# Fixed places for every tile in a two-layer decode kernel: three slots and a ring, a half-wise feed-forward, and 192 KB kept across the layers

## The chip, the core and the metric

The kernel runs on one core of a Trainium2 chip. TensorE (PE in the profile) multiplies, VectorE (DVE), ScalarE (ACT) and GpSimd (POOL) do the rest, and SyncE (SP) issues nearly all loads from HBM into the on-chip memory, which has 128 partitions. Sixteen DMA engines carry them. A "KB" below is a KB per partition unless "in all" stands beside it. The metric is the device time of one execution in microseconds; less is better.

## The reference

Two batch rows, one new token each, go through attention with a long cache, a gated feed-forward, and then through both a second time with the same weights and caches. Everything is float32.

```
B, Sq, D = 2, 1, 512;  Hq, Hkv, Sk, Dh = 32, 8, 32768, 128;  F = 1792
A(x): q = (x @ wq) as 32 heads; k, v repeated 4 times over the heads
      p = softmax(q . k * Dh**-0.5);  o = p . v;  return o @ wo
B(x): gate = x @ W_gate; up = x @ W_up; gate = gate * (gate > 0)
      return (gate * up) @ W_down
x = A_x
x = x + A(layernorm(x));  x = x + B(layernorm(x))
x = x + A(layernorm(x));  x = x + B(layernorm(x))
```

The keys take 268 MB and the values 268 MB, and each of the two layers reads them, so that nearly all bytes are caches.

## The kernel before, in words

A layer has 16 turns, one for each pair of a key head and a batch row (`NG`). A turn has a key half and a value half of 128 KB each. Either is cut in 8 pages of 16 KB, and 4 pages are one slot of 64 KB. `keys(i)` (L394) multiplies the queries with the 8 key pages of turn i (`k_tile`, L218, 8 products of 512 columns for a page), `soft_max` (L226) and `soft_tail` (L241) make the weights and turn them, and `values(i)` (L419) multiplies them with the 8 value pages (`v_tile`, L297 to L309) into one PSUM tile, `acc`. `evacuate` (L313) scales and copies it, `head_out` (L322) folds it into `oT`, and every second turn `project` (L331) multiplies a pair of heads with 8 KB of `wo` into the PSUM tile `op`, in 16 products of 128 columns (`spread`, L164). The program order is keys(i), then values(i-1) (L456 to L458), so the loads of a turn's keys are issued ahead of the values of the turn before. Layer 0 takes the turns upward and layer 1 downward: the last turn of layer 0 is the first of layer 1, and its keys (128 KB) and 56 KB of its values (pages 4, 5, 6 and half of page 3, `KEPT_PAGES` and `KEPT_PART`, L37 and L38) stay on the chip.

All data lie in one tile of 221 KB, `arena`, cut in units of 1 KB. `take` (L62) hands out a run of free units: for a load the one that has been free longest by the program's order, for a working tile the one nearest the top. So where a tile lies follows from the whole order of takes and `done` calls (L79). A load waits on SP until the last reader of its units has finished, and all later loads stand behind it on SP's queue. Most cache loads are whole slots (`pages`, L94, with `whole`); the values of turns 14 and 15 and some pages at the layers' border come as single pages (L437 to L438), the last page of turn 15 in four pieces of 4 KB.

The side load: of turn 14's page 3 the last 3 of 8 column blocks (6 KB) are not loaded with the page. They come from an array `side`, packed as rows, by two DMAs of 20 partitions with 20 KB each, whose source has an outermost dimension of 5 (`load_side`, L288 to L293, `SIDE_ENGINES`, L44). `side_keys` (L258) regroups the weights for it and `v_side` (L276) multiplies 10 chunks. The load is issued after page 3 and ahead of page 4 (L446 to L449).

Between the layers the work is one chain: the last value pieces, `evacuate`, `head_out`, `project` (L463), the addition to x (`add`, L168), then `feed_forward` (L337): `centred` (L143), 8 loads of 7 KB of gate and up weights with products of 448 columns (L345), `variance` (L153, four products), the gate's relu on ACT (L356), product and transposes on DVE, then 6 loads of down weights (8, 8, 4, 4, 2, 2 KB; `DOWN`, L39), whose first 8 blocks go into a PSUM tile of their own, `dn` (L371), that is copied (L378) and folded into `tot` (L381). `queries` (L175) of the next layer follows, with 8 loads of 8 KB. Its products are interleaved with the first products of the kept keys (L190). The free space for all these loads is what the 184 KB kept leave. At the end of layer 1 nothing is kept, and the weights are loaded ahead into free slots.

Of the kernel before, what the change touches and what calls it, by code (L numbers as in the profile page):

```python
# [12 lines left out]
P = 128  # L13
D = 512
# [12 lines left out]


PIECE = 256
PAGE = 4096  # L30
HALF = 4
UNITS = 221
TOP = 192
SCRATCH = 64


KEPT_PAGES = (4, 5, 6)  # L37
KEPT_PART, KEPT_FROM = 3, 4  # L38
DOWN = (4, 4, 2, 2, 1, 1)  # L39


SIDE_TURNS = (14,)
SIDE_PAGE, SIDE = HALF - 1, 3
SIDE_ENGINES, SIDE_ROWS, SIDE_CHUNKS, SIDE_GAP = 5, 20, 5, 64  # L44
# [5 lines left out]
def attention_reglu_decode(ctx: ExitStack, tc: tile.TileContext, x, k, v, wq, wo, wgu, wd, consts, side, out):  # L50
# [6 lines left out]

    arena = sb.tile([P, UNITS * PIECE], F32, name="arena")
    freed = [0] * UNITS
    clock = [0]  # L60

    def take(width, top=True, tile=True):  # L62
        n = -(-width // PIECE)
        step = min(8, 1 << (n - 1).bit_length()) if n < 64 else n
        runs = [
            (top and u < TOP, 0 if tile else max(freed[u : u + n]), -u if n < 16 else u, u)
            for u in range(0, UNITS - n + 1, step)
            if None not in freed[u : u + n]
        ]
        u = min(runs)[-1]  # L70
        freed[u : u + n] = [None] * n
        return arena[:, u * PIECE : u * PIECE + width], range(u, u + n)

    def load(src, top=False):
        t = take(src.shape[-1], top, False)
        nc.sync.dma_start(t[0], src)
        return t

    def done(loaded):  # L79
        clock[0] += 1  # L80
        for u in loaded[1]:
            freed[u] = clock[0]


    def blocks(src, size, order, per):
        for at in range(0, len(order), per):
            t, us = load(src[:, order[at] * size : (order[at] + per) * size])
            for e in range(per):
                yield t[:, e * size : (e + 1) * size], us if e == per - 1 else ()

    def page(src, n, j):
        return load(src[n, j // HALF, :, j % HALF * PAGE : (j % HALF + 1) * PAGE])

    def pages(src, n, whole):  # L94
        for h in range(NT // HALF):
            if whole:
                t, us = load(src[n, h])
                for j in range(HALF):
                    yield t[:, j * PAGE : (j + 1) * PAGE], us[16 * j : 16 * j + 16]
            else:  # L100
                for j in range(HALF):
                    yield page(src, n, HALF * h + j)


# [17 lines left out]
    nc.gpsimd.memset(qz, 0.0)  # L122
    qT = sb.tile([P, HKV * REP, NB], F32, name="qT")
# [8 lines left out]
    ring = sb.tile([P, 32], F32, name="stat")  # L132
    turn = [0]

    def one(n=1):
        at = turn[0]
        turn[0] = (at + 2) % 32
        return ring[:, at : at + n]

    def centred(total, name):  # L143
        mp = small(f"mean{name}")
        nc.tensor.matmul(mp[:, :32], total.to_broadcast([P, P]), means, start=True, stop=True)  # L145
        xT, sq = take(P), take(P)
        nc.vector.transpose(xT[0], xq)
        rows = xT[0].rearrange("p (a b) -> p a b", b=32)
        nc.vector.tensor_tensor(rows, rows, mp[:, None, :32].to_broadcast([P, KT, 32]), ALU.subtract)
        nc.vector.tensor_tensor(sq[0], xT[0], xT[0], ALU.mult)  # L150
        return xT, rows, sq

    def variance(sq, name):  # L153
        vp = small(f"var{name}")
        for kt in range(KT):
            nc.tensor.matmul(vp[:, :NB], mean.to_broadcast([P, P]), sq[0][:, kt * 32 : kt * 32 + NB],
                             start=kt == 0, stop=kt == KT - 1)
        done(sq)
        ve = one(NB)
        nc.vector.tensor_scalar_add(ve, vp[:, :NB], EPS)  # L160
        return ve

# [10 lines left out]


    def queries(L, total, first, between):  # L175
        xt, xT, sq = centred(total, f"a{L}")
# [3 lines left out]
        order = [B * KT + kt for B in (front, 1 - front) for kt in range(KT)]  # L180
        parts = blocks(wq, 4 * D, order, 1 if L else 2 * KT)
        for B in (front, 1 - front):
            for kt in range(KT):
                t = next(parts)
                for c in range(4):
                    nc.tensor.matmul(qp[32 * c : 32 * c + 32, B, :], xT[:, kt, :], t[0][:, c * D : (c + 1) * D],  # L186
                                     start=kt == 0, stop=kt == KT - 1)
                done(t)
                if B != front and kt:
                    next(between, None)  # L190
                if B == front and kt == 0:
                    ve = variance(sq, f"a{L}")
                    nc.gpsimd.tensor_tensor(rq, ve, mhalf, ALU.pow)
                    nc.vector.tensor_scalar_mul(rq, rq, DH ** -0.5)
            q = take(D)
            qs = q[0].rearrange("p (a b) -> p a b", b=32)
            nc.vector.transpose(q[0], qp[:, B, :])
            for b in range(NB):
                nc.vector.tensor_scalar_mul(qT[:, 16 * B : 16 * B + 16, b], qs[:, :, b], rq[:, b : b + 1])
            done(q)  # L200
            if B == front:
                place_queries(0, first)
        done(xt)
# [4 lines left out]

# [16 lines left out]

    def soft_max(L, n):  # L226
# [3 lines left out]
        mt = take(32)  # L230
        nc.vector.tensor_scalar_mul(mt[0], pair, m1[:, 0:1])  # L231
        nc.tensor.matmul(mp[:, :32], same, mt[0], start=True, stop=True)  # L232
        done(mt)
        nm = one()
        nc.vector.tensor_reduce(nm, mp[:, :32], AX.X, ALU.max, negate=True)  # L235
        p = take(2 * D)
        rs = one()
        nc.scalar.activation(p[0], sc_of[n].rearrange("p a b -> p (a b)"), AF.Exp, bias=nm[:, 0:1], scale=1.0, accum_out=rs)  # L238
        red_of[n] = (p, rs)

    def soft_tail(L, n, aside=False):  # L241
        p, rs = red_of.pop(n)
        pT = take(2 * D)
        for B in range(2):
            nc.vector.transpose(pT[0][:, B * D : (B + 1) * D], p[0][:, B * D : (B + 1) * D])  # L245
        if aside:
            side_of[n] = side_keys(p[0])
        done(p)
# [8 lines left out]

    def side_keys(p):  # L258
        W = SIDE_CHUNKS * 32
        t = take(2 * W)  # L260
        at = SIDE_PAGE // 2 % 2 * D + (SIDE_PAGE % 2 * 8 + 8 - SIDE) * 32

        def windows(rows):
            return bass.AP(rows.tensor, rows.offset + at, [rows.ap[0], [SIDE_ROWS, SIDE_CHUNKS], [1, 32]])

        def chunks(rows):
            return rows.rearrange("p (k r) -> p k r", r=32)

        nc.gpsimd.memset(t[0][64:, W:], 0.0)
        nc.vector.transpose(chunks(t[0][:, :W]), windows(p))  # L270
        for c in (0, 32):
            nc.vector.transpose(chunks(t[0][c : c + 32, W:]), windows(p[64 + c : 96 + c]))
        nc.vector.tensor_scalar_mul(t[0], t[0], side_rows[:, 0:1])
        return t

    def v_side(n, vt):  # L276
        t = side_of.pop(n)
        J = SIDE_PAGE // 4
        for k in range(2 * SIDE_CHUNKS):
            nc.tensor.matmul(  # L280
                acc[32 * (k % 4) : 32 * (k % 4) + 16, :],
# [108 lines left out]
    for L in range(NLAYER):  # L390
# [3 lines left out]
        def keys(i):  # L394
# [8 lines left out]
            for j, t in enumerate(loads):  # L403
# [5 lines left out]
                if last and i == 0:  # L409
                    yield  # L410
# [112 lines left out]
```

## Time and profile before

| | |
|---|---|
| median of 3 runs | 2583.39 us (2583.19 to 2585.2) |
| profiled execution: its own time, its span | 2585.52 us, 2583.7 us |
| instructions in the trace | 20190 |
| PE, DVE, ACT busy | 1322.4, 148.4, 40.9 us |
| HBM read | 1105.39 MB, 428 GB/s over the span |
| granted TensorE clock, mean | 0.746 |

The span is what the profiler saw of the program's instructions; the execution's own time is 1.8 us longer. Each query of the trace gives rows. A row of the timeline has the start and length in us, the engine and line, the operation, its output and inputs, the number of instructions merged, and in brackets the idle time before them and what ended it. "SPq" is SP's queue of issues. A row of the windows has the bounds and the length, the busy time of each engine with its instructions, the granted clock, the share of time in which the 16 DMA engines were busy, and what they moved. Every float32 product counts as two matmul instructions.

### The profile page before, as it was taken

What the parts mean: (1) busy time and instruction counts of PE and PEld (TensorE: products, weight loads), DVE (VectorE), ACT (ScalarE), POOL (GpSimd) and SP (SyncE); (2) the same over time, 40 slices, a digit from 0 to 9 for tenths busy, and PEclk for the clock granted to TensorE, in tenths of its full rate; (3) what the DMA queues carried; (4) which work ended last, traced back from release to release, by engine and by line L of the source; (5) the groups of instructions that cost most, each with busy time, mean ns of one, the idle gap of its engine ahead of it and who ended that gap; (6) DMA issues with size and microseconds to landing.
All of it is one profiled execution on the core that took longest, in us unless ns stands there. A gap on an engine that the chain in (4) does not pass through costs nothing.

```text
span 2583.7 us, 20190 instructions
## 1 busy us (share of the span) xinstructions
PE 1322.4 (51%) x9588; PEld 351.7 (14%) x9588; DVE 148.4 (6%) x357; ACT 40.9 (2%) x67; POOL 2.4 (0%) x10
## 2 busy tenths in 40 slices
PE   3554554455455445545685454445445544554465
PEld 1111111111111111111121111111111111111111
DVE  0000000000000000000010000000000000000000
ACT  0000000000000000000000000000000000000000
POOL 0000000000000000000000000000000000000000
PEclk9777777777777777777777777777777777777787
DMA  9999999999999999999999999999999999999999
GB/s 423 436 426 433 436 430 433 437 428 435 431 436 427 436 437 427 434 434 403 414 387 438 428 433 435 434 430 436 431 430 437 433 426 437 435 430 434 431 424 376
DMA packets 31446, 1106.75 MB, mean 428 GB/s; under 512 B 3500, under 2 KB 3764, under 8 KB 6836
## 3 DMA queue, kind: packets, MB, share of 16 engines
q1 hardware_dynamic: 31204, 1105.34, 99.5%
q8 instruction: 75, 1.23, 0.2%
q10 hardware_dynamic: 160, 0.12, 0.0%
q14 instruction: 7, 0.06, 0.0%
HBM read 1105.39 MB, written 0.07 MB: 428 GB/s over the span
## 4 chain that ended last, share of the span: by engine, by line
DMA 69%; PE 22%; another core or an unknown queue 8%; DVE 0%; issue 0%; ACTq 0%; SPq 0%; POOL 0%; DVEq 0%; POOLq 0%
DMA arena<-k 45%; DMA arena<-v 21%; PE sc L218 14%; PE acc L304 5%; DMA cst<-consts 1%; DMA arena<-wgu 1%; PE qp L186 1%; PE po L326 1%; DMA arena<-wq 1%; PE op L166 1%; PE gu L345 0%; PE dn L371 0%; PE mp L232 0%; PE sm L250 0%
## 5 line engine op out<-in xcount | busy, mean ns | idle before, releaser
L304 PE MATMUL acc<-arena 128*16 128x512 f32 (+1 forms) x4116 | 593.0, 727 | 598.5 <-DMA arena<-v 598.5
L218 PE MATMUL sc<-arena,qz 128*32 128x512 f32 x4096 | 591.6, 730 | 592.6 <-DMA arena<-k 592.6
L218 PEld LDWEIGHTS sc<-arena,qz 128*32 128x32 f32 x4096 | 143.4, 130 | 987.8 <-issue 664.9
L304 PEld LDWEIGHTS acc<-arena 128*16 128x16 f32 x4116 | 118.5, 109 | 1023.1 <-issue 512.4
L228 DVE TENSOR_REDUCE stat<-sc 128x1 f32<-128x1024 f32 x32 | 39.2, 1225 | 662.4 <-PE sc L218 662.4
L238 ACT ACTIVATE arena<-sc,stat 128x1024 f32<-128x1024 f32 x32 | 35.6, 1113 | 2360.2 <-DVE stat L235 2308.2
L320 DVE TENSOR_SCALAR arena<-acc,stat 128x512 f32<-128x512 f32 (+1 forms) x38 | 24.8, 665 | 810.6 <-PE acc L304 810.6
L245 DVE STREAM_TRANSPOSE arena<-arena 128x512 f32<-128x512 f32 x64 | 41.5, 687 | 2.4 <-ACT arena L238 2.4
L326 PE MATMUL po<-cst,arena 128*128 128x4 f32 x256 | 34.7, 258 | 2.1 <-DVE arena L320 2.1
L326 PEld LDWEIGHTS po<-cst,arena 128*128 128x128 f32 x256 | 31.9, 195 | 26.7 <-issue 23.5
L252 DVE RECIPROCAL stat<-sm 128x1 f32<-128x1 f32 x32 | 5.3, 166 | 415.4 <-PE sm L250 415.4
L345 PE MATMUL gu<-arena 128*32 128x448 f32 x128 | 22.7, 836 | 9.5 <-DMA arena<-wgu 9.2
L235 DVE TENSOR_REDUCE stat<-mp 128x1 f32<-128x32 f32 x32 | 6.1, 191 | 350.1 <-PE mp L232 350.1
L186 PE MATMUL qp<-arena 128*32 128x512 f32 x128 | 22.7, 822 | 5.7 <-DMA arena<-wq 3.0
L166 PE MATMUL op<-arena,oT 128*2 128x128 f32 x512 | 18.3, 287 | 4.1 <-DVE oT L329 4.1
L232 PEld LDWEIGHTS mp<-arena,cst 128*128 128x128 f32 x64 | 13.1, 256 | 52.1 <-issue 49.6
L145 PE MATMUL meana<-cst,stat 128*128 128x32 f32 x4 | 1.0, 341 | 35.5 <-DMA cst<-consts 35.0
L232 PE MATMUL mp<-arena,cst 128*128 128x32 f32 x64 | 16.9, 353 | 3.5 <-DVE arena L231 3.5
L250 PEld LDWEIGHTS sm<-stat,cst 128*128 128x128 f32 x64 | 9.5, 188 | 28.4 <-issue 28.4
L166 PEld LDWEIGHTS op<-arena,oT 128*2 128x2 f32 x512 | 12.3, 87 | 6.4 <-DVE oT L329 5.5
L250 PE MATMUL sm<-stat,cst 128*128 128x1 f32 x64 | 12.2, 260 | 0.0
L329 DVE COPY oT<-po 128x4 f32<-128x4 f32 x32 | 5.1, 161 | 76.4 <-PE po L326 76.4
(56 smaller groups left out, 94.1 us busy)
## 6 DMA issues: line engine op xcount, KB each, us to landing
arena<-v SPq DMA_DIRECT2D x31, 2048.0 KB, 27.7
arena<-wo SPq DMA_DIRECT2D x16, 1024.0 KB, 51.2
arena<-k SPq DMA_DIRECT2D x8, 2048.0 KB, 16.8
arena<-wq SPq DMA_DIRECT2D x8, 1024.0 KB, 8.5
arena<-wgu SPq DMA_DIRECT2D x8, 896.0 KB, 7.9
arena<-wgu SPq DMA_DIRECT2D x4, 1792.0 KB, 21.0
arena<-v SPq DMA_DIRECT2D x8, 512.0 KB, 34.2
arena<-wd SPq DMA_DIRECT2D x4, 1024.0 KB, 8.7
```

Source lines behind the costliest of these rows:

```text
L166: nc.tensor.matmul(tot[32 * c : 32 * c + rows.shape[-1], :P], rows, w[:, c * P : (c + 1) * P], start=start, stop=stop)
L186: nc.tensor.matmul(qp[32 * c : 32 * c + 32, B, :], xT[:, kt, :], t[0][:, c * D : (c + 1) * D], start=kt == 0, stop=kt == KT - 1)
L218: nc.tensor.matmul(sc_of[n][32 * c : 32 * c + 32, B, :], qz[:, i % 2, 28 - 4 * j : 60 - 4 * j], kt[:, ch * D : (ch + 1) * D], start=j == 0 ...
L228: nc.vector.tensor_reduce(m1, sc_of[n], AX.XY, ALU.max)
L232: nc.tensor.matmul(mp[:, :32], same, mt[0], start=True, stop=True)
L238: nc.scalar.activation(p[0], sc_of[n].rearrange("p a b -> p (a b)"), AF.Exp, bias=nm[:, 0:1], scale=1.0, accum_out=rs)
L245: nc.vector.transpose(pT[0][:, B * D : (B + 1) * D], p[0][:, B * D : (B + 1) * D])
L250: nc.tensor.matmul(sm[:, 0:1], same, rs, start=True, stop=True)
L304: nc.tensor.matmul(acc[32 * c : 32 * c + 16, e * w : (e + 1) * w], pT[:, B, m, 16 * J : 16 * J + 16], vt[:, at * D + e * w : at * D + (e + ...
L320: nc.vector.tensor_scalar_mul(acs[:, at : at + w], acc[:, at : at + w], linv[:, 0:1])
L326: nc.tensor.matmul(po[:, :REP], acs[0][:, t * P : (t + 1) * P], selh[:, 4 * t : 4 * t + 4], start=t == 0, stop=t == 3)
L345: nc.tensor.matmul(gu[32 * j : 32 * j + 32, s, :FS], xT[:, kt, :], t[0][:, j * FS : (j + 1) * FS], start=kt == 0, stop=kt == KT - 1)
```

## The change

The allocator is gone, and each tile has a written place. Units 0 to 191 are three slots of 64 KB, taken in rotation by whole loads, and units 192 to 220 are a ring of 29 KB with one fixed place for each working tile. `home(s, p)` is a page's place in a slot. The other parts:

- Kept across the layers: pages 3 to 6 whole (64 KB) beside the 128 KB of keys. All three slots are then full, and the weights between the layers (`wgu`, `wd`, `wq`, the last `wo`) stream through the ring alone, in places that come round every three loads.
- The values of turns 13, 14 and 15 come as pages; in layer 0, turns 14 and 15 use one slot for both halves. The second key half of turn 15 comes in two loads of 32 KB.
- The side load moves to turn 13 and comes as four DMAs of 25 partitions with 8 KB each, one for each 32 partitions, again with an outermost dimension of 5; its place is ring units 16 to 23. Four chunks are multiplied, not ten.
- `project` makes 4 products of 512 columns for the first 7 pairs; `gather` folds their sum once a layer.
- `feed_forward` works in two column halves: gate and up of half 0, its relu, product and transposes, then half 1; the down weights go straight into `tot` (8, 6, 8, 4, 2 KB), and `variance` is one product after the gate and up products.

The diff, cut: most removed lines stand in the listing above.

```diff
+KB = 256
+SLOT, RING, ARENA = 64, 192, 221
+KEPT_PAGES = (3, 4, 5, 6)
+DOWN = ((4, 3), (4, 2, 1))
+SIDE_TURN = NG - 3
+SIDE_PAGE, SIDE = 3, 3
+SIDE_WAYS, SIDE_ROWS, SIDE_CHUNKS, SIDE_GAP = 5, 25, 4, 64
...
+    def take_slot():
+        s = next_slot[0]
+        next_slot[0] = (s + 1) % 3
+        return s
+
+    def whole(src, n, cut=1):
         for h in range(NT // HALF):
...
+            s, m = take_slot(), cut if h else 1
+            for e in range(m):
+                t = load(slot(s, e * SLOT // m, HALF * PAGE // m), src[n, h, :, e * HALF * PAGE // m : (e + 1) * HALF * PAGE // m])
+                for j in range(HALF // m):
+                    yield t[:, j * PAGE : (j + 1) * PAGE]
...
+    P_AT, ACS_AT, SIDE_KEYS_AT, SUM_AT, SIDE_AT, WO_AT, MT_AT, XT_AT = 8, 12, 14, 14, 16, 20, 28, 28.5
+    G_AT, H_AT, HT_AT, SQ_AT, Q_AT, LAST_ACS_AT = 0, 0.875, (1.75, 2.625), 3.5, 0, 4
+    LAST_AT = (4, 8, 12, 16)
+    GU_AT = ((6, 13, 20, 6), (13, 20, 6, 13))
+    DOWN_AT = ((20, 6), (12, 20, 24))
+    WQ_AT = (4, 8) + (12, 20, 4) * 3
+
+    def pT_at(i):
+        return 0 if i % 2 else 4
...
+    nc.gpsimd.memset(ring(P_AT, (WO_AT + 8 - P_AT) * KB), 0.0)
...
+        for at, (B, kt, cs, t) in enumerate(blocks):
+            if t is None:
+                lo = (B * KT + kt) * 4 * D + cs[0] * D
+                t = load(ring(WQ_AT[at], len(cs) * D), wq[:, lo : lo + len(cs) * D])
...
+    def v_side(L, n):
+        vt = ring(SIDE_AT, SIDE_CHUNKS * D)
+        for c in range(4):
+            load(vt[32 * c : 32 * c + SIDE_ROWS],
+                 side[L, c, :, : SIDE_ROWS // SIDE_WAYS * SIDE_CHUNKS * D].rearrange("e (r f) -> e r f", r=SIDE_ROWS // SIDE_WAYS))
+        t, J = side_of.pop(n), SIDE_PAGE // 4
+        for k in range(SIDE_CHUNKS):
             nc.tensor.matmul(
...
+    def project(pair_at, w, final):
         for u in range(REP):
...
+            if final:
+                spread(op, oT[:, u, :], w[:, u * D : (u + 1) * D], False, u == REP - 1)
+            else:
+                nc.tensor.matmul(op[32 * u : 32 * u + NB, :], oT[:, u, :], w[:, u * D : (u + 1) * D],
+                                 start=pair_at == 0, stop=pair_at == HKV - 2)
+
+    def gather():
+        t = ring(SUM_AT, D)
+        nc.vector.tensor_copy(t, op)
+        for c in range(4):
+            nc.tensor.matmul(op[32 * c : 32 * c + NB, :P], sel[:, :NB], t[:, c * P : (c + 1) * P], start=True, stop=False)
+
+    def feed_forward(L, total, spare):
+        xT, ss = centred(total, f"f{L}")
+        hT = []
+        for half in range(2):
+            gu = ps.tile([P, 2, D], F32, tag="sc", bufs=2, name=f"gu{L}_{half}")
+            many = 1 if spare is None else 2
+            for at in range(0, KT, many):
+                width = many * 2 * 4 * HF
+                lo = (half * KT + at) * 2 * 4 * HF
+                t = load(ring(GU_AT[half][at], width) if spare is None else slot(spare[0], (half * KT + at) * 7, width),
+                         wgu[:, lo : lo + width])
...
+            nc.scalar.activation(g, gu[:, 0, :HF], AF.Relu)
+            nc.vector.tensor_tensor(h, gu[:, 1, :HF], g, ALU.mult)
+            nc.vector.transpose(hT[half], h)
+        ve, by_row, r2 = variance(ss, f"f{L}"), one(NB), one()
...
+        for half in range(2):
+            rows = hT[half].rearrange("p (a b) -> p a b", b=32)
+            for at, n in enumerate(DOWN[half]):
+                place = ring(DOWN_AT[half][at], n * D) if spare is None else slot(spare[1], 2 * c, n * D)
+                t = load(place, wd[:, c * D : (c + n) * D])
+                for e in range(n):
+                    spread(tot, rows[:, c - half * HC, :], t[:, e * D : (e + 1) * D], c == 0, c == NC - 1)
+                    c += 1
...
+            elif L and i == 1:
+                loads = (load(home(key_slots[j // HALF], j % HALF), part(k, n, j, 0, 8)) for j in range(NT))
...
+                if i == NG - 1:
+                    key_slots[:] = [next_slot[0], (next_slot[0] + 1) % 3]
+                loads = whole(k, n, 2 if i == NG - 1 else 1)
...
+            if i >= SIDE_TURN:
+                if i == SIDE_TURN or last:
+                    pages_at[:] = [take_slot(), take_slot()]
+                elif i == SIDE_TURN + 1:
+                    pages_at[:] = pages_at[1:] * 2
+                pieces = [(j, 0, 8, home(pages_at[j // HALF], j % HALF)) for j in range(NT)]
...
+                if i == NG - 1:
+                    pieces[NT - 1 :] = [(NT - 1, 2 * e, 2 * e + 2, ring(at, 2 * D)) for e, at in enumerate(LAST_AT)]
```

More of the change, by code (lines that the diff above doesn't have):

```diff
@@ L54, in attention_reglu_decode @@
     ctx.enter_context(tc.manual_schedule())
[L58 to L72, printed above, removed]
@@ L91, in page @@
-    def page(src, n, j):
-        return load(src[n, j // HALF, :, j % HALF * PAGE : (j % HALF + 1) * PAGE])
-    def pages(src, n, whole):
-        for h in range(NT // HALF):
[L96 to L102, printed above, removed]
+    arena = sb.tile([P, ARENA * KB], F32, name="arena")
@@ L179, in queries @@
         front = first // (NG // 2)
[L180 to L202, printed above, removed]
```

307 lines of the change are left out of this document (129 added, 178 removed).

## The prediction

> **What bounds the kernel now.** I read the page first, then windows by stage, then the timeline where a window showed the DMA engines idle.
>
> ```profile
> span 2583.7 us, 20190 instructions
> PE 1322.4 (51%) x9588; PEld 351.7 (14%) x9588; DVE 148.4 (6%) x357; ACT 40.9 (2%) x67; POOL 2.4 (0%) x10
> q1 hardware_dynamic: 31204, 1105.34, 99.5%
> ```
>
> SP's queue q1 fills the 16 DMA engines for 99.5% of the span, and PE is busy for half of it. So nearly every microsecond is bytes, and a change can win in three ways: fewer bytes, a better rate, or less idle time of the DMA engines. The windows give the rates and the idle places (columns: bounds and length, busy time and instructions of PE, its weight loads, DVE, ACT, POOL, then clock, DMA share, GB/s):
>
> ```profile
> 72.00:1160.00 1088.00, 538.04 (x3874) 141.83 (x3874) 56.78 (x127) 18.07 (x30) 0.23 (x1) 0.73 1.00 433
> 1218.60:1222.20 3.60, 3.33 (x30) 0.77 (x22) 1.17 (x3) 1.20 (x2) 0.00 (x0) 1.00 0.53 224
> 1289.50:1292.00 2.50, 1.40 (x16) 0.84 (x12) 1.11 (x4) 0.00 (x0) 0.00 (x0) 0.85 0.58 211
> 1368.00:1386.00 18.00, 10.40 (x62) 2.03 (x66) 0.00 (x0) 0.00 (x0) 0.00 (x0) 0.74 1.00 425
> 2495.00:2541.00 46.00, 25.36 (x158) 5.30 (x155) 2.08 (x5) 0.00 (x0) 0.00 (x0) 0.85 1.01 428
> 2571.50:2576.50 5.00, 3.48 (x24) 0.79 (x20) 1.27 (x2) 0.00 (x0) 0.00 (x0) 0.50 0.81 333
> 1290.19:1363.71 73.52, 59.20 (x449) 19.11 (x449) 12.45 (x40) 1.75 (x3) 0.69 (x1) 0.74 0.97 386
> ```
>
> Whole slots come at 433 GB/s with no idle time; pages of 16 KB come at 425 to 428, also with none. Idle time stands in layer 0's side stage (1218.6), at the layers' border (1289.5, and on average over the last row) and at the end. At 1218.6 the share is 0.53: about 8 of 16 engines work while 8 wait. At the end it is 0.81, 13 of 16. The engines do not run level, then: half are ahead by some microseconds, and a tile is complete only when the last of the 16 has landed its part. Idle time of the engines ahead costs little by itself.
>
> **The side stage.** The timeline there, in layer 0, and then the same place in layer 1:
>
> ```profile
> 1221.10 1.70 SPq L292 DMA_DIRECT2D arena<-side  x2
> 1226.98 1.89 PE L304 MATMUL acc<-arena 128*16 128x512 f32 x10 [1.18 <-DMA arena<-v]
> 1231.28 2.76 PE L280 MATMUL acc<-arena 128*16 128x512 f32 x20 [2.41 <-DMA arena<-side]
> 1236.08 3.11 PE L304 MATMUL acc<-arena 128*16 128x512 f32 x16 [2.04 <-DMA arena<-v]
> 1240.97 1.91 PE L304 MATMUL acc<-arena 128*16 128x512 f32 x8 [1.78 <-DMA arena<-v]
> ...
> 2456.01 1.53 SPq L292 DMA_DIRECT2D arena<-side  x2
> ...
> 2491.67 1.46 PE L304 MATMUL acc<-arena 128*16 128x512 f32 x9 [1.18 <-DMA arena<-v]
> 2496.73 1.91 PE L304 MATMUL acc<-arena 128*16 128x512 f32 x16 [0.59 <-DMA arena<-v]
> ```
>
> In layer 0, page 3 is used at 1226.98 and page 4 at 1236.08, 9.10 us later. In layer 1 the same step takes 2496.73 - 2491.67 = 5.06 us, and the page after it in layer 0 comes after 4.89. So layer 0 loses 9.10 - 5.06 = 4.04 us. The reason is on SP's queue:
>
> ```profile
> SPq L292 <- PE acc L304: 2.1, 1, 2.1
> ```
>
> The allocator gave layer 0's side load units that pages of the current turn still held, so SP stood until PE had multiplied them, to 1221.10, with pages 4 to 7 queued behind. In layer 1 the load went out at 2456.01, 35.7 us ahead of its page. The wait lets the engines ahead run dry, and the side load then falls on a few of them when their lead is spent. I read "a few" as five, from the outermost dimension of 5 and from the 13 of 16 that end layer 1 late (the 8 slow ones and five). The late ones then keep everything late up to the border: at 1289.5 again only 0.58 of the engines work while PE waits for the last value piece.
>
> In the new kernel the side load has ring units 16 to 23. Their last reader is the projection a full turn earlier, so SP does not wait, and the load stands behind page 3 in the DMA queues long before it is due, as it did in layer 1. The five engines take 20 packets of 8 KB for 8 of 20 KB, the same bytes. **Term 1: -4.0 us.** The lead at turn 13 is a turn younger than at turn 14 and may be short of the load; from the 9.10 us I allow up to 1.5 us back: -4.0 to -2.5. Four chunks for ten on PE (20 instructions to 8, 2.76 us to about 1.1) lie beside page loads of 4.9 us.
>
> **The border.** From the last value product of layer 0 to the fourth key page of layer 1 (the bounds of the 73.52 us window):
>
> ```profile
> 1290.19 0.62 PE L304 MATMUL acc<-arena 128*16 128x256 f32 x8 [0.62 <-DMA arena<-v]
> 1293.42 1.89 PE L166 MATMUL op<-arena,oT 128*2 128x128 f32 x32 [0.26 <-DVE oT L329]
> 1296.77 1.72 PE L345 MATMUL gu<-arena 128*32 128x448 f32 x8 [0.38 <-DVE arena L149]
> 1298.42 1.87 PE L156 MATMUL varf<-arena,cst 128*128 128x2 f32 x8
> 1300.22 4.71 PE L345 MATMUL gu<-arena 128*32 128x448 f32 x24
> 1363.71 1.92 PE L218 MATMUL sc<-arena,qz 128*32 128x512 f32 x16 [0.76 <-DMA arena<-k]
> ```
>
> In between come wo 8, wgu 56, wd 28, wq 64 and four key pages 64 KB, 220 KB or 28.84 MB in all. At 425 GB/s that is 67.9 us, so 5.6 us are lost now. The new kernel loads the same, through a ring of 29 KB for 37 KB before. I walk it with T = 1290.19. A place is free when PE has read it; how soon it can be full again I bound by two rows:
>
> ```profile
> out<-x SPq DMA_DIRECT2D x1, 64.0 KB, 1.6
> DMA to landing us min/median/max: 6.1/7.0/7.9
> ```
>
> A small DMA on empty queues takes 1.6 us, and 7 KB (0.92 MB) at 425 GB/s 2.2, so 3.8 us at least; the wgu loads issued between 1290.8 and 1292 took 6.1 at the best, some of it behind other loads. Since I count only time in which the queues are empty, I take 3.8, and keep 6.1 for a rival. At T the queues hold wo and two wgu pieces, 22 KB or 6.6 us. The third waits for the projection to leave unit 20: 1293.42 + 1.89 is T + 5.1, so it lands at T + 8.9 against T + 8.8 unhindered. The fourth waits for PE's first gate and up block: that starts at T + 6.6 (1296.77) and takes 1.7, so it lands at T + 12.1 against 11.1: 1.0 lost. After that a place comes round in 1.6 (24 instructions in 4.71 are three blocks) + 3.8 = 5.4 us, while the other places keep the queues busy: three loads of 7 KB last 6.5, three of 8 KB 7.4. No further loss until the first key page, whose place waits for two blocks of PE; I put 0.6 there. The `variance` products (1.87 us) no longer stand between the first two blocks. Lost after: 1.6 us, a gain of 4.0. But the walk is for a mean engine and PE waits for the last of 16, so I count half of it. **Term 2: -2.1 us**, from -4.0 to +3.
>
> **Bytes and cuts.** 8 KB more kept are 1.05 MB in all less; at 433 GB/s **term 3 is -2.4 us**. The loads are cut finer: the rows of the issues show 31 value and 8 key pages now, with whole slots without a size:
>
> ```profile
> arena<-v SPq DMA_DIRECT2D x31, 2048.0 KB, 27.7
> arena<-k SPq DMA_DIRECT2D x8, 2048.0 KB, 16.8
> ```
>
> By the code the pages become 48 and 8: 17 more pages, 35.7 MB, at 427 for 433 GB/s, 83.6 for 82.4 us. **Term 4: +1.2 us**; with the 32 KB loads 0.9 to 1.5.
>
> [...]
>
> **One slot for two halves.** In layer 0, page j + 4 of turn 14 waits on SP until PE has read page j, with the rest queued behind it. Three pages, 14.7 us, are then in the queues; PE needs 1.9 to 3.1 us for a page (the rows at 1240.97 and 1236.08) and a DMA 1.6 us to start. Cost nothing, with some 10 us of cover; without the cover each page would cost those 5 us.
>
> **The end.** Layer 1's weights go ahead into free slots, so the queues stay full to the last down block. After it:
>
> ```profile
> 2575.41 3.23 PE L371 MATMUL dn<-arena 128*32 128x512 f32 x16 [1.52 <-DVE arena L360]
> 2578.70 0.69 DVE L378 COPY arena<-dn 128x512 f32<-128x512 f32 x1 [3.39 <-PE dn L371]
> 2579.69 1.06 PE L166 MATMUL tot<-arena 128*32 128x128 f32 x32
> 2580.81 0.35 DVE L170 SCALAR_TENSOR_TENSOR x<-tot,stat,x 128x128 f32<-128x128 f32 x1 [1.42 <-PE tot L166]
> ```
>
> PE, not the load, ends last: the product into `dn` waits for the whole of h, then the copy, the fold, and four blocks in 1.06 us. In the new order half 0's seven blocks run early, copy and fold are gone, and one block of 8 instructions (0.27 us) is left when the last load lands. If that load had landed when PE began the four, 0.8 of the 1.06 us go; if it came later, or half 1 keeps PE late, less. **Term 5: -0.5 us** (-0.8 to 0).
>
> **Free of cost.** The wider output products (32 instructions of 128 columns to 8 of 512) and `gather` lie under key loads. The memset of 20 KB is on POOL at the start, before the first softmax. DVE's added sum of squares stands beside gate and up products. If PE's cover at the border is short, the price is in term 2's upper end.
>
> **Sum.** -4.0 - 2.1 - 2.4 + 1.2 - 0.5 = -7.8 us. The profiled execution took 2585.5 us (span 2583.7), 2.1 more than the median 2583.4; the new one then takes 2577.7 profiled and **2575.6 us** in the median.
>
> **The rivals.**
> - *The ring is too short* (slower). If a place needs 6.1 us to fill after PE's 1.6, a round of three takes 7.7 us against 6.5 to 7.4, about 0.8 lost in each of 7 rounds, 5.6 us: term 2 becomes +1.6, and 2579.3. It decides the sign when a round takes over 9 us, as with PE blocks of 3 us: some 2 us in each of 7 rounds make term 2 +14 - 4 = +10, the sum +4.3, and 2587.7; beyond 9.2 us it is over 0.2% slower. For it: the ring is 8 KB shorter and every load waits for PE. Against: PE's blocks here took 1.6 to 1.7 us. Chance 0.06.
> - *Each added DMA pays its fixed part* (slower). 15 more at the 1.6 us of the small DMA make +24, so +16.2 and 2599.6. For it: stages of pages run at a lower rate than whole slots. Against: at 425 for 433 GB/s a page costs 0.09 us more, not 1.6. [...] Chance 0.01.
> - *The side wait only moves* (no change that can be told). If five engines have too little lead at turn 13, or the first page of a shared slot stalls, term 1 is about -1 and term 2 about 0: -2.7 us, 2580.7. For it: the same five engines, the same bytes. Against: layer 1's 5.06 us. Chance 0.18.
> - *All idle time goes* (faster still). Term 1 at -4.0, term 2 at -5.6, term 5 at -0.8: -11.6 us, 2571.8. For it: engines that are not held up at the side stage come to the border level. Chance 0.08.
> - *The kept pages are loaded all the same*: the code takes them from `kept_v`; nothing for it, and the bytes will tell.
>
> **How the numbers follow.** About 0.2%, 5.2 us, is what a measurement of this kernel tells from no change, so the border is at 2578.2. My forecast, -5.3 to -10 us, has 0.67. Faster: 0.67 + 0.08 = 0.75; same 0.18; slower 0.06 + 0.01 = 0.07. The range takes in the forecast, most of the rival on top and the side wait's figure: 2571 to 2581.
>
> **What would show it.** The HBM bytes should be 1.05 MB less. In layer 0, turn 13, page 4 should follow page 3 (and the side products) within about 5.2 us; a gap of 8 or more makes term 1 wrong. From the last value product of layer 0 to the fourth key page I expect 71 to 72 us; over 77 is the short ring, under 69 the larger gain. After the last weight load, the addition to x should come within about 0.7 us, with no copy. A DMA share under 0.99 in the stages of turns 13 to 15 would mean that the single slot stalls.

## The result and the profile after

The changed kernel takes 2597.21 us in the median of 4 runs (2595.7 to 2597.66), the kernel before beside it 2583.29 us (2581.61 to 2585.2). The ratio is 1.0053, with a 95% interval of 1.0035 to 1.0070: slower by half a per cent, where 2575.6 us and a gain had been forecast. The profiled execution took 2597.25 us. From the page of the changed kernel, the busy times, the DMA rate in 40 slices, the queue and the bytes:

```profile
span 2595.4 us, 19909 instructions
PE 1329.1 (51%) x9428; PEld 347.6 (13%) x9428; DVE 148.0 (6%) x361; ACT 41.3 (2%) x69; POOL 6.2 (0%) x9
...
GB/s 421 435 436 432 430 434 432 436 430 431 432 435 433 435 431 429 437 391 428 409 344 439 428 433 432 434 435 431 430 436 435 434 427 433 433 435 426 394 428 382
...
q1 hardware_dynamic: 32928, 1104.30, 99.6%
...
HBM read 1104.34 MB, written 0.07 MB: 426 GB/s over the span
```

The bytes fell by 1.05 MB as forecast, and the queue is as busy as it was, yet the rate fell. Three places show in the slices: 391 (layer 0) and 394 (layer 1), which are the side stages, and 344, the border. The windows of these places (columns as in the prediction), with undisturbed stages between them:

```profile
72.00:1120.00 1048.00, 519.75 (x3608) 133.71 (x3600) 55.99 (x126) 18.16 (x29) 0.00 (x0) 0.73 1.00 433
1138.00:1151.00 13.00, 8.39 (x59) 1.62 (x52) 1.39 (x3) 1.21 (x2) 0.00 (x0) 0.86 1.03 273
1152.00:1290.00 138.00, 77.73 (x499) 17.02 (x495) 6.72 (x14) 1.21 (x2) 0.00 (x0) 0.77 1.00 425
1291.05:1373.32 82.27, 59.85 (x540) 22.23 (x540) 12.32 (x43) 1.92 (x4) 0.70 (x1) 0.69 0.95 354
...
2400.00:2426.00 26.00, 19.21 (x131) 4.41 (x124) 1.66 (x3) 1.21 (x2) 0.00 (x0) 0.76 1.01 339
```

In both side stages the engines count as busy all the time (share 1.03 and 1.01) and move 273 and 339 GB/s. So the time is not idle time of the DMA engines: transfers are under way and go slowly. The timeline of layer 0's side stage in the changed kernel:

```profile
1098.19 30.16 SPq L65 DMA_DIRECT2D arena<-side  x4
...
1132.58 17.38 SPq L65 DMA_DIRECT2D arena<-v  x4
...
1137.48 1.89 PE L275 MATMUL acc<-arena 128*16 128x512 f32 x16
1139.64 1.91 PE L275 MATMUL acc<-arena 128*16 128x512 f32 x16
1143.60 3.45 PE L275 MATMUL acc<-arena 128*16 128x512 f32 x16 [2.06 <-DMA arena<-v]
1149.61 2.61 PE L275 MATMUL acc<-arena 128*16 128x512 f32 x10 [2.56 <-DMA arena<-v]
...
1151.62 2.31 PE L261 MATMUL acc<-arena 128*16 128x512 f32 x8
...
1156.20 2.40 PE L275 MATMUL acc<-arena 128*16 128x512 f32 x16 [2.27 <-DMA arena<-v]
...
1161.09 3.48 PE L275 MATMUL acc<-arena 128*16 128x512 f32 x16 [2.49 <-DMA arena<-v]
```

Two of the four side DMAs go out at 1098.19, some 40 us ahead. SP then stands 8.3 us before the third (1108.24) and 18.7 us before the fourth (1127.63), both times until a load of keys has landed, and page 4 goes out at 1132.58. These waits do not explain the slow stretch: pages 0 to 3 had all gone out by 1098.14, page 4 went out 23.6 us before its use, and the DMA share is 0.95 to 1.08 in every 4 us from 1128 to 1152. Yet page 3, of which only 10 KB are loaded, comes 6.01 us after page 2, and page 4 after another 6.59, where whole pages outside the stage follow each other in 4.89 (1156.20 to 1161.09).

The border in the changed kernel, from the last value product to the fourth key page, and the page's rows of the weight loads (median us from issue to landing at the end of the row):

```profile
1291.09 0.63 PE L275 MATMUL acc<-arena 128*16 128x256 f32 x8 [0.63 <-DMA arena<-v]
...
1301.17 1.72 PE L330 MATMUL gu<-arena 128*32 128x224 f32 x16 [0.92 <-DMA arena<-wgu]
1305.02 1.72 PE L330 MATMUL gu<-arena 128*32 128x224 f32 x16 [2.13 <-DMA arena<-wgu]
...
1373.36 1.92 PE L210 MATMUL sc<-arena,qz 128*32 128x512 f32 x16 [0.40 <-DMA arena<-k]
```

```profile
arena<-wgu SPq DMA_DIRECT2D x8, 896.0 KB, 6.6
arena<-wq SPq DMA_DIRECT2D x7, 1024.0 KB, 7.1
```

It takes 82.27 us, 8.75 more than before. Before, PE waited for no load in its first four gate and up blocks and 0.5 to 1.6 us in each of the last four; now it waits 0.3 to 2.5 us for every load from the third on. The end:

```profile
2590.17 2.25 PE L157 MATMUL tot<-arena 128*32 128x128 f32 x56 [1.64 <-DMA arena<-wd]
2592.00 0.16 PEld L157 LDWEIGHTS tot<-arena 128*32 128x32 f32 x8 [0.27 <-DMA arena<-wd]
2592.49 0.35 DVE L161 SCALAR_TENSOR_TENSOR x<-tot,stat,x 128x128 f32<-128x128 f32 x1 [4.83 <-PE tot L157]
```

So the difference can be laid out by three rows: the last value product of layer 0 is 0.90 us later (1290.19 to 1291.09), the border 8.75 longer, and the way from the fourth key page to the addition to x 2.03 longer (1217.10 to 1219.13). The sum, 11.68, is the difference of the spans. Layer 0 should have come 4 us earlier and layer 1 should have saved bytes, so behind the two small numbers stand larger losses.

### The profile page after: what moved, and what is told of

The parts are those of the page before. It is cut to its first block, busy times and chain, and to the rows that moved or that the text cites. A ratio compares the mean times of both kernels' runs of the same rounds, so it can differ in the third digit from the quotient of the medians.

```text
span 2595.4 us, 19909 instructions
## 1 busy us (share of the span) xinstructions
PE 1329.1 (51%) x9428; PEld 347.6 (13%) x9428; DVE 148.0 (6%) x361; ACT 41.3 (2%) x69; POOL 6.2 (0%) x9
## 3 DMA queue, kind: packets, MB, share of 16 engines
q1 hardware_dynamic: 32928, 1104.30, 99.6%
## 4 chain that ended last, share of the span: by engine, by line
DMA 66%; PE 23%; another core or an unknown queue 11%; issue 0%; SPq 0%; DVE 0%; ACTq 0%; POOL 0%; POOLq 0%; DVEq 0%
DMA arena<-k 50%; PE sc L210 15%; DMA arena<-v 11%; PE acc L275 5%; DMA arena<-wd 1%; DMA cst<-consts 1%; DMA arena<-side 1%; DMA arena<-wo 1%; DMA arena<-wgu 1%; PE qp L181 1%; PE po L295 1%; DMA arena<-wq 1%; PE op L306 1%; PE mp L223 0%
## 5 line engine op out<-in xcount | busy, mean ns | idle before, releaser
L275 PE MATMUL acc<-arena 128*16 128x512 f32 (+1 forms) x4116 | 601.2, 733 | 591.9 <-DMA arena<-v 591.8
L210 PE MATMUL sc<-arena,qz 128*32 128x512 f32 x4096 | 599.3, 738 | 593.7 <-DMA arena<-k 593.7
L330 PE MATMUL gu<-arena 128*32 128x224 f32 x256 | 22.0, 494 | 16.6 <-DMA arena<-wgu 16.1
L306 PE MATMUL op<-arena,oT 128*2 128x512 f32 x112 | 14.6, 592 | 3.6 <-DVE oT L297 3.6
L157 PE MATMUL tot<-arena 128*32 128x128 f32 x224 | 11.3, 367 | 5.8 <-DMA arena<-wd 5.4
L330 PEld LDWEIGHTS gu<-arena 128*32 128x32 f32 x256 | 9.4, 140 | 28.0 <-DMA arena<-wgu 16.1
```

The source lines that it names most:

```text
L210: nc.tensor.matmul(sc_of[n][32 * c : 32 * c + 32, B, :], qz[:, i % 2, 28 - 4 * j : 60 - 4 * j], kt[:, ch * D : (ch + 1) * D], start=j == 0 ...
L275: nc.tensor.matmul(acc[32 * c : 32 * c + 16, e * w : (e + 1) * w], pT[:, B, m, 16 * J : 16 * J + 16], vt[:, at * D + e * w : at * D + (e + ...
L306: nc.tensor.matmul(op[32 * u : 32 * u + NB, :], oT[:, u, :], w[:, u * D : (u + 1) * D], start=pair_at == 0, stop=pair_at == HKV - 2)
L330: nc.tensor.matmul(gu[32 * j : 32 * j + 32, s, :HF], xT[:, at + e, :], t[:, f : f + HF], start=at + e == 0, stop=at + e == KT - 1)
```

## The experiments

Two theories were formed from these traces. **Places:** the side load is carried by five engines (the author's estimate, as in the prediction, from its outermost dimension of 5 and a DMA share of 0.81; no row shows the engines one by one), and the partitions on which its rows now stand slow it and the pages beside it. That other engines write these partitions in the page loads, and that the engines then hold each other up, was the author's supposition and is not shown. **Ring:** a place in the 29 KB ring takes longer to come round than the other places keep the queues busy. The rivals: the position in turn 13, the pages, the finer cuts. All ratios are to the kernel before, timed on the same chip beside them (2583.95 us for e1 to e4, 2583.27 for e5 to e8, 2583.91 for e9 to e11).

| run | median us | ratio, 95% interval |
|---|---|---|
| e1_no_side | 2590.50 | 1.0024 (1.0013 to 1.0035) |
| e2_side_2x20 | 2586.93 | 1.0013 (1.0004 to 1.0023) |
| e3_side_4x20 | 2595.10 | 1.0043 (1.0028 to 1.0058) |
| e4_before_side64 | 2597.46 | 1.0049 (1.0032 to 1.0066) |
| e5_kept184 | 2589.57 | 1.0025 (1.0015 to 1.0034) |
| e6_both | 2579.95 | 0.9985 (0.9977 to 0.9994) |
| e7_before_shift4 | 2595.92 | 1.0047 (1.0033 to 1.0060) |
| e8_before_kept192 | 2590.25 | 1.0027 (1.0018 to 1.0036) |
| e9_before_turn13 | 2581.46 | 0.9989 (0.9979 to 0.9998) |
| e10_side_2x20 | 2586.57 | 1.0011 (1.0001 to 1.0020) |
| e11_before_kept176 | 2582.88 | 0.9996 (0.9987 to 1.0006) |

**e1, no side load.**

```diff
-                if i == SIDE_TURN:
-                    pieces[SIDE_PAGE] = (SIDE_PAGE, 0, 8 - SIDE, home(pages_at[0], SIDE_PAGE % HALF, (8 - SIDE) * D))
...
-                if i == SIDE_TURN and j == SIDE_PAGE:
-                    v_side(L, n)
```

> The changed kernel without the side load: page 3 of turn 13 comes whole, nothing else differs. In the changed kernel, between 1138 and 1151 us of layer 0, the DMA engines were busy (share 1.03) and moved 273 GB/s; value pages came 6.0 to 6.6 us apart there instead of 4.9, in both layers, some 12 us over what the same pages cost elsewhere. Theory A (the side load itself slows the engines: its rows stand where five engines must write beside others): without it that stretch goes at 425 to 428 GB/s with pages 4.9 us apart; page 3 whole costs some 2 us a layer; time about 2587 to 2590. Rival B (the slow stretch belongs to turn 13's order, its pages of 16 KB in shared places or the young lead of the engines): the stretch stays at under 350 GB/s and the time at 2595 to 2599. The border between the layers, 82.3 us from the last value product to the fourth key page, stays at 81 to 83 in either.

The same window of this kernel:

```profile
1138.00:1151.00 13.00, 8.74 (x66) 1.65 (x58) 1.40 (x3) 1.21 (x2) 0.00 (x0) 0.87 1.00 427
```

427 GB/s for 273: the slow stretch belongs to the side load and not to the turn or its pages. The median, 2590.5, is just above the range of theory A. The border, 79.87 us, stays long, though a little under the 81 to 83 expected.

**e2 and e10, the old rows in the new turn.**

```diff
-SIDE_WAYS, SIDE_ROWS, SIDE_CHUNKS, SIDE_GAP = 5, 25, 4, 64
+SIDE_WAYS, SIDE_ROWS, SIDE_CHUNKS, SIDE_GAP = 5, 20, 5, 64
...
-    P_AT, ACS_AT, SIDE_KEYS_AT, SUM_AT, SIDE_AT, WO_AT, MT_AT, XT_AT = 8, 12, 14, 14, 16, 20, 28, 28.5
+    P_AT, ACS_AT, SUM_AT, SIDE_AT, WO_AT, MT_AT, XT_AT = 8, 12, 14, 8, 20, 28, 28.5
...
+        vt = ring(SIDE_AT, 2 * SIDE_CHUNKS * D)
+        for c in range(2):
             load(vt[32 * c : 32 * c + SIDE_ROWS],
```

In e2 the side keys stood in a slot that a key load then filled, so that its side products multiply other numbers and that load stands behind the keys. Both runs have two DMAs of 20 partitions with 20 KB each, as the kernel before, where the change has four of 25 with 8 KB, and ten chunks for four. In e10 the side keys stand beside the shortened page 3.

> The changed kernel with the old layout of the side rows (20 rows on each of two row groups, 0 to 19 and 32 to 51, ten chunks, the same bytes from the same five pieces), still in turn 13 and without a wait on SP. Theory A (where the rows stand and how many each engine writes decides): pages 4.9 to 5.2 us apart, the stretch at 420 GB/s or more, time about 2585 (2583 to 2587). Rival B (position in turn 13 or the load on five engines decides, whatever the rows): pages stay 6 us apart, 2595 to 2599. Rival C (the old layout only has the 4 us that layer 0 lost before): about 2589 to 2591.

> The changed kernel with the old layout of the side rows (20 rows on partitions 0 to 19 and 32 to 51, ten chunks), in turn 13, the side keys now in the half-empty page place where nothing overwrites them, which the run e2_side_2x20 had not. Place theory: value pages of turn 13 come 4.9 to 5.3 us apart, the stretch of 1138 to 1151 moves 420 GB/s or more, and the time is 2585 to 2588, as e2_side_2x20 gave (2586.9), some 10 us under the changed kernel; the border stays at 80 us or more. Rival (e2_side_2x20 was fast for another reason, since it used other numbers and held a key page): 2592 or more.

```profile
1138.00:1151.00 13.00, 9.80 (x76) 2.38 (x68) 1.27 (x3) 1.21 (x2) 0.00 (x0) 1.00 1.01 428
2400.00:2426.00 26.00, 15.86 (x132) 3.51 (x121) 1.66 (x3) 1.21 (x2) 0.00 (x0) 1.00 1.00 426
...
1286.34 0.63 PE L288 MATMUL acc<-arena 128*16 128x256 f32 x8 [0.63 <-DMA arena<-v]
```

With the same bytes in two DMAs for four, and on partitions 0 to 19 and 32 to 51 alone, both stages of e10 go at full rate and the median falls by 10.6 us (2597.21 to 2586.57); e2 gave nearly the same. The last value product comes at 1286.34, 4.75 earlier than in the changed kernel and 3.85 earlier than before. The border stays at 81.80 us. That is theory A's outcome; but the number and the size of the DMAs changed with the partitions, so e10 by itself does not tell them apart. e4 and e7 do.

**e3, four groups of 20 rows.**

```diff
-SIDE_WAYS, SIDE_ROWS, SIDE_CHUNKS, SIDE_GAP = 5, 25, 4, 64
+SIDE_WAYS, SIDE_ROWS, SIDE_CHUNKS, SIDE_GAP = 5, 20, 5, 64
```

> The changed kernel with four row groups as in the change but 20 rows in each and five chunks: each of the five engines writes four rows of a group, not five, so that its rows are aligned to groups of four partitions. Rows 64 to 83 and 96 to 115 are still used. Theory A1 (rows on partitions 64 and up are what slows): about half the loss stays, the stretch at 300 to 390 GB/s, pages 5.3 to 6 us apart, 2588 to 2593. Theory A2 (only the five rows, out of step with groups of four, slow it): no loss, about 2585. Rival B (neither): 2595 to 2599. [...]

```profile
1138.00:1151.00 13.00, 6.13 (x46) 1.34 (x50) 0.19 (x1) 1.21 (x2) 0.00 (x0) 0.87 1.02 312
```

The rate is between the ends, as A1 had it, but the time is not: 2595.1 is 2.1 us under the changed kernel and 8.5 over e10. So the five rows, out of step with groups of four, are at most a small part (the intervals of the two runs overlap). The 8.5 us stand for half of the rows on partitions 64 and up and for four DMAs in place of two, which e3 does not separate. "About half" was too low, and the lower end of rival B was reached; by the time alone B would stand. What decides against it is e10 with e4.

**e4 and e7, the kernel before with its side rows elsewhere.** The loads of e4, and those of e7; the weights for the rows move with them.

```diff
-            nc.sync.dma_start(t[0][32 * c : 32 * c + SIDE_ROWS],
+            nc.sync.dma_start(t[0][64 + 32 * c : 64 + 32 * c + SIDE_ROWS],
```

```diff
-            nc.sync.dma_start(t[0][32 * c : 32 * c + SIDE_ROWS],
+            nc.sync.dma_start(t[0][32 * c + SIDE_AT : 32 * c + SIDE_AT + SIDE_ROWS],
+SIDE_AT = 4
```

> The kernel before with one thing changed: its side rows stand on partitions 64 to 83 and 96 to 115 instead of 0 to 19 and 32 to 51. Same bytes, same packets, same turn, same order. Theory A1 (a load that five engines carry slows when its rows stand on partitions that other engines write): in layer 1, where the load is issued early, page 4 follows page 3 after 7 us or more instead of 5.06, and the time rises by 4 to 12 us, to 2587 to 2595. Rival (the rows per engine, or the packets of 8 KB, are what slowed the changed kernel, and the partitions do not matter): 5.0 to 5.3 us and 2582 to 2585.

> The kernel before with its side rows four partitions further: 4 to 23 and 36 to 55 instead of 0 to 19 and 32 to 51. [...] Theory A (an engine that writes into partitions that another engine writes in the pages shares a way into memory with it, and both slow): the time rises as with rows 64 and up, to 2588 to 2598, and layer 1's page 4 follows page 3 after 7 us or more. Rival U (the upper 64 partitions are slow for these engines, neighbours are not): 2582 to 2585 and 5.0 to 5.3 us. [...]

Windows of 13 us in layer 1's side stage: the kernel before, then e4, then e7.

```profile
2484.00:2497.00 13.00, 10.07 (x80) 2.25 (x76) 1.26 (x3) 1.21 (x2) 0.00 (x0) 1.00 1.01 429
```

```profile
2490.00:2503.00 13.00, 4.75 (x38) 1.13 (x34) 0.71 (x3) 1.20 (x2) 0.00 (x0) 0.79 0.99 219
```

```profile
2490.00:2503.00 13.00, 6.13 (x42) 1.31 (x42) 0.34 (x2) 1.20 (x2) 0.00 (x0) 0.87 1.00 352
```

And the pages 1 to 4 of that turn in e7:

```profile
2490.55 1.91 PE L305 MATMUL acc<-arena 128*16 128x512 f32 x16
2496.38 3.41 PE L305 MATMUL acc<-arena 128*16 128x512 f32 x16 [3.91 <-DMA arena<-v]
2502.75 2.07 PE L305 MATMUL acc<-arena 128*16 128x512 f32 x9 [2.96 <-DMA arena<-v]
...
2508.43 2.20 PE L305 MATMUL acc<-arena 128*16 128x512 f32 x16
```

These two settle that the partitions by themselves slow the stage. Nothing differs but the partitions of the rows and of their weights, and the kernel before loses 13.5 us (2583.95 to 2597.46, 2.5 above the range of theory A1) and 12.7 us (2583.27 to 2595.92). In e7 the rows moved by four partitions within the same half, so it is not that the upper half is slow: rival U falls. Where the loss shows was foretold wrongly: page 4 follows page 3 after 5.68 us in e7 (4.90 in e4), not 7; it shows ahead of that, at pages 2 and 3 (5.83 and 6.37 us in e7, 10.16 us for page 2 in e4, against 4.89 for a page outside the stage). Why 352 GB/s in e7 cost nearly as much as 219 in e4 was not shown; no run here shows the engines one by one.

The places of the rows and the rates, side by side: on partitions 0 to 19 and 32 to 51 the stage moves 429 GB/s (before, layer 1) and 428 (e10, layer 0), on 4 to 23 and 36 to 55 352 (e7, layer 1), on 64 to 83 and 96 to 115 219 (e4, layer 1), in four groups of 20 312 (e3, layer 0) and in four groups of 25 273 (the changed kernel, layer 0). So e4 and e7 show that the partitions decide. Why they do was not shown: no row tells which engine writes which partition.

**e5, a fourth place at the border.** Half of page 3 is not kept, and its 8 KB serve the weight loads.

```diff
-KEPT_PAGES = (3, 4, 5, 6)
+KEPT_PAGES = (4, 5, 6)
+KEPT_PART, KEPT_FROM = 3, 4
...
-    GU_AT = ((6, 13, 20, 6), (13, 20, 6, 13))
-    DOWN_AT = ((20, 6), (12, 20, 24))
-    WQ_AT = (4, 8) + (12, 20, 4) * 3
+    HALF_AT = 100
+    GU_AT = ((HALF_AT, 6, 13, 20), (HALF_AT, 6, 13, 20))
+    DOWN_AT = ((HALF_AT, 6), (12, 20, 24))
+    WQ_AT = (HALF_AT, HALF_AT + 4) + (4, 12, 20, HALF_AT) * 2
```

> The changed kernel with half of page 3 (8 KB) no longer kept for layer 1; those 8 KB serve as a fourth place for the weight loads between the layers, so four places turn where three did. The side load is as in the change. Ring theory (in the changed kernel a place comes round in 8.3 to 9.0 us while three loads of 7 KB last 6.5): four places hold 8.7 us of loads, so from the last value product of layer 0 to the fourth key page of layer 1 it should take 73 to 76 us instead of 82.3; 1.05 MB more cost 2.4 us; time about 2591 to 2593. Rival (the border is late because the side load has put the engines out of step, or because the weights come in smaller cuts): the border stays over 80 us and the time rises to 2598 or more.

```profile
1290.97:1362.83 71.86, 53.16 (x540) 19.42 (x540) 12.32 (x43) 1.92 (x4) 0.69 (x1) 0.83 0.98 403
```

71.86 us for 82.27, a larger gain than expected, with the side load, the cuts and the column halves as in the change. The median falls by 7.6 us, to under the range, although 1.05 MB more are read. The ring theory holds, and the rival falls.

**e8 and e11, the kernel before with 8 KB more kept, and 8 KB less.** One number each: `KEPT_PART, KEPT_FROM = 3, 4` becomes `3, 8`, with pages 3 to 6 in `KEPT_PAGES` (e8) or 4 to 6 (e11).

> The kernel before with 8 KB more kept (192 KB, as in the change), its allocator and its order as they are, so that 8 KB less are free for the weights between the layers. Ring theory: the border grows from 73.5 us to 76 to 82, the bytes save 2.4 us, time 2583 to 2590. Rival (the border of the changed kernel is long for another reason, its written places or its column halves): the border stays within 72 to 74.5 us and the time falls to 2580 to 2582.

> The kernel before with 8 KB less kept (176 KB), so 8 KB more are free at the border. Ring theory in the other direction: if the kernel before still waits for places there, the border goes from 73.5 us to 70 to 72 and pays back up to the 2.4 us that 1.05 MB more cost, time 2582 to 2584. Rival (at 184 KB the border does not wait for places any more): 73 to 74 us and 2585 to 2587.

```profile
1289.09:1369.22 80.13, 60.42 (x448) 17.71 (x448) 12.46 (x40) 1.75 (x3) 0.69 (x1) 0.74 0.95 362
```

```profile
1289.83:1359.12 69.29, 55.76 (x448) 18.07 (x448) 12.45 (x40) 1.75 (x3) 0.70 (x1) 0.80 1.00 408
...
arena<-wgu SPq DMA_DIRECT2D x8, 896.0 KB, 13.4
```

With its own allocator and order, the kernel before goes from 69.29 us at 176 KB kept to 73.51 at 184 and 80.13 at 192. So places at the border limit it too, and the 8 KB more that the change keeps would have lost more (6.6 us) than their bytes save (2.4). The median of e8 rose by 7.0 us, to just above its range; its profiled execution, 2587.62 us, was one of its fastest, so 6.6 may be low. In e11 the border fell more than the 70 to 72 expected, and gain and bytes nearly cancel: the interval holds 1. The last row shows that the time from issue to landing is no constant of a load: in e11 it is 13.4 us for 7 KB, with 8 KB more room for the loads, while the border is the shortest of all.

**e9, the kernel before with its side load in turn 13.** `SIDE_TURNS = (14,)` becomes `(13,)`.

> The kernel before with one thing changed: its side rows (old places on partitions 0 to 19 and 32 to 51) belong to turn 13 in layer 0, not 14. Theory of term 1 (the wait for units held by pages of the turn is what cost layer 0 4.0 us): if the units are free earlier at turn 13, SP does not stand, page 4 follows page 3 after about 5 us, the last value product of layer 0 comes at about 1286 instead of 1290.2, and the time is 2579 to 2580. Rival (the younger lead of the engines at turn 13 is short of the load, or the allocator's wait only moves along): the last value product stays at 1289 to 1291 and the time at 2582 to 2584.

```profile
1286.37 0.63 PE L304 MATMUL acc<-arena 128*16 128x256 f32 x8 [0.38 <-DMA arena<-v]
```

3.82 us earlier at that row, as term 1 had it. The median falls by 2.45 us, less than the expected 4 and between the ranges of theory and rival, with an interval of 0.5 to 5.4; the two profiled spans differ by 3.9, and the row decides for the theory.

**e6, both remedies** (the diffs of e10 and e5 together).

> The changed kernel with both remedies: the side rows on partitions 0 to 19 and 32 to 51 (the old layout, in turn 13) and the fourth 8 KB place at the border. If the two causes are separate and together all of it, the border takes 73 to 76 us, value pages of turn 13 come 4.9 to 5.3 us apart, and the time is 2579 to 2582, below the kernel before by 2 to 4 us (the side wait of layer 0 gone, the shorter end, and the finer cuts to pay). If there is a third cause, 2584 or more.

```profile
1286.20:1357.87 71.67, 55.37 (x540) 20.78 (x540) 12.32 (x43) 1.92 (x4) 0.69 (x1) 0.76 0.99 404
1138.00:1151.00 13.00, 8.60 (x68) 2.25 (x64) 0.19 (x1) 1.20 (x2) 0.00 (x0) 1.00 1.01 429
```

2579.95 us, 17.3 under the changed kernel; the two remedies by themselves gave 10.6 and 7.6. They nearly add up, a third cause of that size is not there, and this version is faster than both kernels, by 0.15% (0.06 to 0.23) against the one before.

## Why the prediction was wrong

**Term 1 (-4.0).** Right in the wait, wrong in the load. The wait was longer than the quoted 2.1 us: SP had first stood 42.4 us until a load of values had landed. The wait went, and it was worth 3.8 us (e9 at the last value product; e10 3.85). The step that failed is "The five engines take 20 packets of 8 KB for 8 of 20 KB, the same bytes": it looked at bytes, pieces and due times and not at which partitions each piece writes. That cost 10.6 us over both layers (e10; in its profile 4.75 up to the last value product and 6.38 from the fourth key page to the addition to x), and it was in none of the rivals: "the same five engines, the same bytes" was even put forward in one of them. The sign I had set, a gap of 8 us from page 3 to page 4, did not appear (6.59); the loss was spread over three pages, so one gap was too narrow a sign. "SP does not wait" was wrong too, as SP stood 8.3 and 18.7 us between the side DMAs, but no loss is seen from it. How much the four smaller DMAs cost beside the partitions was not measured.

**Term 2 (-2.1, up to +3).** Wrong in sign: +8.75. The step that failed is "I take 3.8": the time to fill a place again, made from the store of the result on empty queues and the bytes. Under the loads of this ring it is 6.6 us for 7 KB and 7.1 for 8 KB (medians of the profile's page), and the row quoted in the prediction had already said 6.1 at the best. With PE's 1.7 us a place comes round in 8.3 to 8.8 us, against 6.5 to 7.4 for three loads. The reason given for the lower value, that only time with empty queues counts, does not hold: with loads under way 95% of the time the border moved 354 GB/s, not 425. What the 6.6 us are made of (the load ahead, the last of the engines) was not taken apart. The rival "the ring is too short" had the mechanism: "some 2 us in each of 7 rounds" are 14 us, and 82.27 less the 67.9 that the bytes need are 14.4. That its figure fits is partly luck, as it got there by PE blocks of 3 us, while PE's stayed at 1.7 and the fill was what was longer. Its chance of 0.06 was too low, and halving the gain for the last of 16 engines does not help where the sign is wrong. A small slip in the walk, 6.6 us for 22 KB where 425 GB/s make it 6.8, changes nothing.

**Term 3 (-2.4).** The 1.05 MB are gone. From the fourth key page to the addition to x, 1.05 MB more to read make the way 2.53 us longer in e5 than in the changed kernel (1221.66 for 1219.13), 2.14 longer in e11 than before (1219.24 for 1217.10) and 4.54 longer in e6 than in e10 (1217.29 for 1212.75), so 2.4 is about right.

**Term 4 (+1.2).** The pages of turns 14 and 15 come at 425 GB/s and whole slots at 433, as assumed. e6 bears it out roughly: -3.8 for the wait, -1.8 for its border (71.67 for 73.51), +1.2 and -0.5 make -4.9, and -3.3 was measured, with an interval of -1.6 to -5.9; the +1.2 by itself was not measured.

**One slot for two halves (nothing).** Right: 1152 to 1290 has a DMA share of 1.00 and moves 425 GB/s, the rate of pages.

**Term 5 (-0.5).** Right: no copy, and the addition starts 0.5 us after the weight load at 2592.00, which waited for the last piece. Before, the last load went out at 2562.30 and landed 17.4 us later, some 1.1 us ahead of the addition (2580.81).

**The rivals.** The traces count 234 loads on SP in the changed kernel and 219 before, 15 more, 4 of them at the side. They did not pay 1.6 us each: e6, with the finer cuts, is faster than before. All idle time did not go. The side wait did not only move: with the old rows it is gone at turn 13 (e9: the last value product 3.82 us earlier), so the load has lead enough there.

With terms 3, 4 and 5 as they were, the true sum is about -3.9 for the wait, +10.6 for the rows' places and +8.75 for the border, -2.4, +1.2, -0.5: +13.8 us, where the medians differ by 13.9. That it comes out to 0.1 us is luck: the sum mixes medians, rows of single profiles and forecasts that were kept, and a profiled execution and the median of its kernel differ by up to 3.2 us (e1).

## What to carry to other kernels

When a load of rows on some of the partitions runs beside full loads, write down which partitions each piece fills, and measure a new place by itself before it goes into a larger change; a shift by four partitions cost 12.7 us in 2583 (e7). Price a ring by an issue-to-landing time that a row shows with about as many loads under way as the ring allows (6.1 to 7.1 us here), not by an idle DMA and the bytes: the number of places times a load's duration must exceed the reader's time plus that (three places of 6.5 to 7.4 us fell short of 8.3 to 8.8 here; with a fourth, in e5, the border took 71.86 us for 82.27). And memory that saves bytes by keeping data may be worth more as a place to stream through: here each 8 KB saved some 2.4 us of bytes and cost 4.2 us (176 to 184 KB kept), 6.6 (184 to 192) and, in the changed kernel, 10.4 us at the border.

## What the runs showed of the hardware

A DMA share of 1.0 did not mean a full rate here. In the disturbed side stages the engines count as busy (0.99 to 1.03) while they move 219 to 352 GB/s for 429, so the share counts a slow transfer as busy too; the 99.6% of the whole queue in the changed kernel hid a loss of 19 us (10.6 and 8.75). At its border, too, the share of 0.95 shows less of the loss than the rate, 354 for 425. The column of GB/s, stage by stage, shows it.

Half of the rows on partitions 64 and up (e3, against e10) cost 8.5 us and all of them there (e4, against the kernel before) 13.5. The two pairs are of different kernels, and e3 has four DMAs for two, so whether the loss goes by the number of rows stays open. Which engines carry the rows, and what slows them at these partitions, was not measured.
